# Where the first spectral fold stands at the seam of two MLP groups

## The chip, the cores and the metric

The kernel runs on one core of one Trainium2 chip. The metric is the device time of one execution in microseconds (us). TensorE does the matmuls, VectorE and ScalarE the element-wise work and all reads of PSUM, GpSimd element-wise work on SBUF, and SyncE issues the DMAs. Each engine works through its own instructions in the order in which they stand in the program. In the profile the engines are PE (with PEld for its weight loads), DVE, ACT, POOL and SP.

## The reference

```python
x = A_x                                    # 1 x 2048 x 448, float32
xn = layernorm(x)
# spectral branch (GFNet): 2-D real FFT, a complex weight, and back
y  = irfft2(rfft2(xn, axes=(-2, -1)) * (A_w_r + 1j * A_w_i), s=(2048, 448), axes=(-2, -1))
# S2-MLP branch
h  = gelu(layernorm(xn) @ w1)              # 448 -> 448
hs = shift(h, +1, -1, +2, -2 on the four channel quarters) @ w2
x1 = xn + hs
h2 = gelu(layernorm(x1) @ w3) @ w4         # 448 -> 1792 -> 448
out = x + y + (x1 + h2)
```

## The kernel before

All matmuls are done in float16 with each operand split into a high half and a low half, three products per matmul of the reference: high by high, high by low, low by high. So every operand is made by two instructions, a ScalarE copy that rounds to the high half, and a VectorE subtraction that leaves the low half. The 2048 tokens are 16 blocks of 128, block b holding the tokens with number b modulo 16, and they are called `xb(b)`.

The program runs in this order. First come the LayerNorm, `w1`, the shift and `w2`, block by block. `ln2` is the second LayerNorm: for a set of up to four blocks it takes statistics, subtracts the mean, scales to a high half (L481, ScalarE) and a low half (L482 and L484, VectorE: two column ranges) in the tile `y`, and transposes each block into `x2all` by a DMA (L486). The last call of it covers blocks 12 to 15.

Then the second MLP. It is cut into units (G, fp): G counts the eight pairs of blocks, fp the seven groups of 256 hidden channels. A unit has a front (`front`): 22 matmuls (L381) of 256 columns into one PSUM bank `pw`, then a gelu in place (L698, ScalarE), the high half `hf` (L700, ScalarE) and the low half (L701, VectorE). And it has a back (`back`): 12 matmuls (L720) of 448 columns into the two `acc` banks, of which 4 use only the high half of `hf` as weights first and the other 8 are placed where the low half is there too. After the seventh back of a G, VectorE adds `acc` to `xb` (L726). Units are queued as filler: `mlp` issues the front of a unit some units ahead of its back (`AH = 2` here), so TensorE always has a front to do while an `hf` is being made. `mlp([0])` forms the first group of units, (0,0) to (0,6); `mlp([1, 2])` the second, (1,0) to (2,6). The fronts use four PSUM banks in turn (tags `mm` and `tr`).

Beside the second group stands the first stage of the spectral branch. It works on eight pairs of blocks b0 = 0, 2, ... 14. `do_fold(b0)` loads the pair again from HBM into `xf` (L509; three buffers), normalizes it (L513, two ScalarE activations), copies one wrap-around column (L514), and lets GpSimd form sums and differences of the row with its mirror image (L519 and L520 into the shared row buffer `xr`, L522 twice into `f`). `step1_in` makes the halves `xh` of each block (L529 ScalarE, L530 VectorE; four buffers). `step1` is the first Fourier product of each block: 12 matmuls of 128 columns (L539) into a bank `ps` (tag `sp`, two buffers), evacuated by L543 (ScalarE) and L544 (VectorE) into `y1`. After all eight pairs the spectral middle (`chunk_a` to `chunk_c`) follows beside the units of G = 2 to 5, then the way back beside the last ones.

A scheduler that models the engines writes out the order of each engine from priorities. The second MLP's matmuls have the lowest priority, the evacuations of `front` the highest. On top of this the program pins instructions with `behind(key)`: what is issued inside may stand on its engine only after the named instruction. Two tables place the folds:

```python
with behind("f", *FOLD[b0 // 2]):      # do_fold: L513, L514 after hf of that unit
    ...
with behind("m", *PACE[b // 2]):       # step1 of both blocks after the back of that unit
    step1(b)
    step1(b + 1)
```

`("f", G, fp)` names L700 and L701 of a unit, `("m", G, fp)` the last matmul of its back. Other uses of the pins at the seam: `unscale` (L491 loads, L492) is pinned behind units of the second group by `EARLY`.

Of the kernel before, what the change touches and what calls it, by code (L numbers as in the profile page):

```python
# [29 lines left out]
VPRE = 2.0 ** -3  # L30
EPS = 1e-5
AH = 2
PACE = [(0, 6), (1, 1), (1, 2), (1, 4), (1, 5), (2, 0), (2, 1), (2, 3)]
FOLD = [(0, 5), (1, 0), (1, 1), (1, 3), (1, 4), (1, 6), (2, 0), (2, 2)]
PIN = [("a3",), ("a3",), ("a3",), ("a3",)]
WMAX = [(1, 4), (1, 5), (1, 6), (2, 0), (2, 1), (2, 2), (2, 3), (2, 4)]
HS = 3
# [82 lines left out]
def body(tc, nc, x, wf, w1, w2, w3, w4, c_g, c_n, c_small, out):  # L120
# [234 lines left out]
    @contextlib.contextmanager  # L355
    def behind(*key):
        key = key if len(key) > 1 else key[0]
        with contextlib.ExitStack() as st:
            for i in after[key]:
                st.enter_context(tc.issue_after(i))  # L360
            yield
# [145 lines left out]
    def do_fold(b0):  # L507
        X = pfd.tile([128, 2, D + 1], F32, tag="xf", bufs=3, name=f"xf{b0}")
        after["X", b0] = (SY.dma_start(X[:, :, 0:D], xv[:, b0:b0 + 2]).ins,)  # L509
        with behind("f", *FOLD[b0 // 2]):  # L510
            for i in range(2):
# [14 lines left out]
    def step1_in(b):  # L526
        f = folds.pop(b)
        t = xh_buf[b % 4]
        i = A.activation(out=t[:, 0:452], in_=f, func=AF.Copy)  # L529
        j = V.tensor_tensor(out=t[:, 452:904], in0=f, in1=t[:, 0:452], op=ALU.subtract)  # L530
        after["x", b] = i.ins, j.ins

    def step1(b):
        t = xh_buf[b % 4]
        pm = bank("sp", f"ps1_{b}")
        for q in range(4):
            for n, (xi, ri) in enumerate(PASS):
                o = xi * 452 + 113 * q
                T.matmul(pm[:, 128 * q:128 * q + 128], t[:, o:o + 128], cR[ri][:, 128 * (q % 2):128 * (q % 2) + 128],  # L539
                         start=n == 0, stop=n == 2)  # L540
        src = pm.rearrange("p (q h k) -> p q h k", h=2, k=4)
        y = [Ya[:, p, :, :, :, b, :].rearrange("p q c h k -> p (q c) h k") for p in range(2)]
        A.activation(out=y[0], in_=src, func=AF.Copy)  # L543
        V.tensor_tensor(out=y[1], in0=src, in1=y[0], op=ALU.subtract)  # L544
# [370 lines left out]
    for b in range(0, NB, 2):  # L915
        do_fold(b)
        step1_in(b)
        step1_in(b + 1)
        with behind("m", *PACE[b // 2]):
            step1(b)  # L920
# [61 lines left out]
```

## Time and profile before

| | |
|---|---|
| median of three runs | 416.20 us (416.14 to 416.21) |
| profiled execution | 416.43 us |
| its span | 414.6 us |
| mean granted TensorE clock | 0.999 of full speed |
| instructions | 8472 |
| matmuls | 3313 |
| bytes read from and written to HBM | 35.52 MB, 3.67 MB |

All times in the trace are counted from the start of the span of the profiled execution; 1.8 us of its time lie outside the span. A row of a timeline gives the start, the length from the first start to the last end, engine, line and operation, what is written from what, the shapes and the number of instructions merged in the row, and in brackets the idle time of the engine before it with what ended it. A row of groups gives the number of instructions, busy time, mean duration in ns, and idle time before them. A row of windows gives for each stretch its length and the busy time and count of PE, PEld, DVE, ACT and POOL, then the clock, the DMA share and the GB/s. A matmul's printed duration overlaps the next one's, so the cost of one is read from starts.

### The profile page before, as it was taken

The page shows a single profiled execution, that of the slowest core. Times are in us where ns is not written, and L with a number is a line of the kernel's source. Part 1 is how long each engine was busy: PE and PEld are TensorE (multiplying, and loading weights), DVE is VectorE, ACT ScalarE, POOL GpSimd, SP SyncE. Part 2 cuts the span into 40 slices and gives each one's busy share as a digit, 9 for nine tenths or more (in the row PEclk, how much of TensorE's full clock was granted, in tenths as well). Part 3 has the DMA queues.
Part 4 walks back from the last instruction along what each step waited for, and adds up shares of the span by engine and source line. Part 5 has one row for each costly group of instructions (what it writes and reads, how often), then busy time and mean ns, then how long its engine had stood idle before and what let it go on. Part 6 is the DMA issues. An engine that isn't in the chain of part 4 may idle for free.

```text
span 414.6 us, 8472 instructions
## 1 busy us (share of the span) xinstructions
PE 407.9 (98%) x3313; PEld 290.4 (70%) x3313; DVE 294.3 (71%) x613; ACT 246.1 (59%) x428; POOL 97.2 (23%) x172
## 2 busy tenths in 40 slices
PE   8999999999989999999999999999999999999996
PEld 3655555765658777776888887877777766777885
DVE  4888899798866879854799888857999934112122
ACT  4698879973758876643689888854344533222321
POOL 3876710102245947400021122110000000000000
PEclk9999999999999999999999999999999999999999
DMA  8959879914867557315256655500111011001001
GB/s 275 350 189 177 159 148 323 158 59 90 186 166 206 153 183 221 90 47 141 70 149 163 168 144 141 127 27 2 69 46 66 2 47 44 2 0 46 2 0 46
DMA packets 54536, 48.53 MB, mean 117 GB/s; under 512 B 37536, under 2 KB 48864, under 8 KB 54496
## 3 DMA queue, kind: packets, MB, share of 16 engines
q1 hardware_dynamic: 54496, 47.99, 43.6%
q8 instruction: 26, 0.43, 0.4%
q14 instruction: 14, 0.11, 0.1%
HBM read 35.52 MB, written 3.67 MB: 95 GB/s over the span
## 4 chain that ended last, share of the span: by engine, by line
PE 68%; DVE 12%; ACT 7%; issue 4%; DMA 4%; POOL 2%; SPq 1%; DVEq 0%; POOLq 0%; ACTq 0%
PE pw L381 26%; PE acc L720 25%; PE pw L410 4%; PE ps L539 3%; PE pe L663 2%; PE wps L749 2%; PE py L684 2%; ACT te L619 2%; DVE xt L452 2%; DMA x2mem<-y 2%; DMA x2mem<-w 1%; PE pu L642 1%; PE pp L597 1%; DVE y L484 1%; PE px L614 1%
## 5 line engine op out<-in xcount | busy, mean ns | idle before, releaser
L381 PE MATMUL pw<-x2mem,w3p 128*128 128x256 f16 x1232 | 151.7, 273 | 0.0
L720 PE MATMUL acc<-w4p,hf 128*128 128x448 f16 (+1 forms) x714 | 139.7, 341 | 1.4 <-DVE hf L701 1.4
L381 PEld LDWEIGHTS <-w3p 128*128 128x128 f16 x1232 | 119.0, 98 | 22.4
L720 PEld LDWEIGHTS <-hf 128*128 128x128 f16 x714 | 69.2, 98 | 49.9 <-DVE hf L701 1.8
L701 DVE SCALAR_TENSOR_TENSOR hf<-pw,h,hf 128x512 f16<-128x512 f32 x56 | 41.8, 747 | 64.1 <-ACT hf L700 63.7
L698 ACT ACTIVATE pw<-pw,pe 128x512 f32<-128x512 f32 x56 | 36.7, 656 | 76.8 <-PE pw L381 76.6
L450 PE MATMUL pw<-w2p,h 112*128 112x448 f16 x192 | 39.9, 352 | 0.7 <-DMA h<-hs 0.7
L700 ACT ACTIVATE hf<-pw,h 128x512 f16<-128x512 f32 x56 | 38.3, 687 | 1.5
L410 PE MATMUL pw<-w1p,xT 128*128 128x448 f16 x176 | 35.4, 352 | 0.0
L623 POOL TENSOR_TENSOR z<-te 128x450 f32<-128x450 f32 x16 | 15.7, 982 | 69.5 <-DVE te L621 69.5
L450 PEld LDWEIGHTS <-h 112*128 112x128 f16 x192 | 18.6, 98 | 17.2 <-DMA h<-hs 1.0
L410 PEld LDWEIGHTS <-xT 128*128 128x128 f16 x176 | 16.9, 98 | 16.4 <-DVE xT L375 0.8
L604 ACT ACTIVATE pf<-pp 64x450 f16<-64x450 f32 x32 | 17.4, 543 | 12.6 <-DVE pf L605 8.3
L605 DVE TENSOR_TENSOR pf<-pp,pf 64x450 f16<-64x450 f32 x32 | 19.9, 622 | 4.3 <-ACT pf L604 3.9
L522 POOL TENSOR_TENSOR f<-xr 128x452 f32<-128x452 f32 x16 | 18.4, 1173 | 0.6
L619 ACT ACTIVATE te<-px 64x450 f32<-64x450 f32 x32 | 17.3, 540 | 1.1 <-PE px L614 0.6
L726 DVE SCALAR_TENSOR_TENSOR xt<-acc,p,xt 128x448 f32<-128x448 f32 (+1 forms) x17 | 10.9, 651 | 8.6 <-PE acc L720 8.3
L530 DVE TENSOR_TENSOR xh<-f,xh 128x452 f16<-128x452 f32 x16 | 12.6, 828 | 5.5 <-ACT xh L529 5.5
L519 POOL TENSOR_TENSOR xr<-xf 128x452 f32<-128x452 f32 x8 | 9.9, 1236 | 26.0 <-issue 20.2
L529 ACT ACTIVATE xh<-f 128x452 f16<-128x452 f32 x16 | 8.4, 571 | 10.3 <-POOL f L522 10.2
L684 PE MATMUL py<-vh,csm 128*128 128x448 f16 x48 | 14.0, 352 | 0.0
L663 PE MATMUL pe<-csm,U 113*128 113x113 f16 (+1 forms) x192 | 13.7, 213 | 0.0
(164 smaller groups left out, 572.5 us busy)
## 6 DMA issues: line engine op xcount, KB each, us to landing
wc<-wf SPq DMA_DIRECT2D x32, 225.0 KB, 3.7
wl<-wf SPq DMA_DIRECT2D x8, 450.0 KB, 4.0
xt<-x SPq DMA_DIRECT2D x8, 448.0 KB, 9.0
xf<-x SPq DMA_DIRECT2D x8, 448.0 KB, 3.9
loads<-x SPq DMA_DIRECT2D x7, 448.0 KB, 3.7
out<-xt SPq DMA_DIRECT2D x13, 224.0 KB, 1.9
w3raw<-w SPq DMA_DIRECT2D x3, 896.0 KB, 13.7
gn<-c_g SPq DMA_DIRECT2D x16, 128.0 KB, 3.1
```

What stands on the lines that cost most here:

```text
L381: T.matmul(ps_out, wp[:, wi + t, cols], xT[:, xi + t, tok], start=t == 0 and wi + xi == 0, stop=t == 3 and wi == 4)
L410: T.matmul(pm[:, :D], xTs[g][:, xi + t, 128 * i:128 * i + 128], w1p[:, wi + t], start=t == 0 and p == 0, stop=t == 3 and p == 2)
L450: T.matmul(pm[:, :D], hT[g][:112, 4 * hi + k, o:o + 128], w2p[:, wi, k], start=n == 0, stop=n == 11)
L522: P.tensor_tensor(out=f[:, :, k:k + 2].rearrange("p b s d -> p s b d"), in0=u[:, :, 0], in1=u[:, :, 1], op=op)
L605: V.tensor_tensor(out=lo, in0=src, in1=hi, op=ALU.subtract)
L619: A.activation(out=e[64 * h:64 * h + 64], in_=px_[64 - 64 * h:128 - 64 * h, :2 * DF], func=AF.Copy)
L663: T.matmul(pe[:, 113 * q:113 * q + 113], U[b // 8 * 8][ui][:kd, q, b % 8, :], cI[ii][:kd, 113 * q:113 * q + 113], start=n == 0, stop=n == 2)
L684: T.matmul(py[:, :D], cV[ri], vh[:, vi], start=n == 0, stop=n == 2)
L698: A.activation(out=pm, in_=pm, func=AF.Gelu_apprx_tanh, scale=r3)
L700: i = A.activation(out=h[:, 0], in_=pm, func=AF.Copy, scale=h3)
L701: j = V.scalar_tensor_tensor(out=h[:, 1], in0=pm, scalar=h3, in1=h[:, 0], op0=ALU.mult, op1=ALU.subtract)
L720: m = T.matmul(to, h[:, hi, o:o + 128], w4p[0][:, wi, f, r], start=f == 0 and n == 0, stop=f == 13 and n == 2)
```

## The change

The first entries of both tables are moved: the fold of blocks 0 and 1 is pinned behind `hf` of unit (0,6), the last unit of the first group, where it was pinned behind that of unit (0,5). The products of these two blocks are pinned behind the back of unit (1,0), the first of the second group, where they were pinned behind the back of (0,6). All the other entries stay.

```diff
-PACE = [(0, 6), (1, 1), (1, 2), (1, 4), (1, 5), (2, 0), (2, 1), (2, 3)]
-FOLD = [(0, 5), (1, 0), (1, 1), (1, 3), (1, 4), (1, 6), (2, 0), (2, 2)]
+PACE = [(1, 0), (1, 1), (1, 2), (1, 4), (1, 5), (2, 0), (2, 1), (2, 3)]
+FOLD = [(0, 6), (1, 0), (1, 1), (1, 3), (1, 4), (1, 6), (2, 0), (2, 2)]
```

## The prediction

> **What bounds the kernel now.** I read the page's busy line and groups first, then the windows, then TensorE's own timeline around the change, then the three engines that feed it there.
>
> ```profile
> PE 407.9 (98%) x3313; PEld 290.4 (70%) x3313; DVE 294.3 (71%) x613; ACT 246.1 (59%) x428; POOL 97.2 (23%) x172
> ```
>
> ```profile
> L381 PE MATMUL pw<-x2mem,w3p 128*128 128x256 f16 x1232 | 151.7, 273 | 0.0
> L720 PE MATMUL acc<-w4p,hf 128*128 128x448 f16 (+1 forms) x714 | 139.7, 341 | 1.4 <-DVE hf L701 1.4
> L381 PEld LDWEIGHTS <-w3p 128*128 128x128 f16 x1232 | 119.0, 98 | 22.4
> ```
>
> TensorE is busy for 98% of the span. The page warns that matmul ends are modelled, so I don't take that share alone as proof; the last column matters more. Of the two largest groups, L381 never finds TensorE idle, and L720 does for 1.4 us in all, waiting for the second half of `hf` (VectorE, L701). The windows say where that is:
>
> ```profile
> 117.96:130.39 12.43, 11.07 (x103) 8.81 (x102) 8.94 (x12) 7.38 (x14) 5.01 (x6) 1.00 0.75 185
> 130.39:215.00 84.61, 84.61 (x783) 64.56 (x781) 64.27 (x94) 54.11 (x96) 35.22 (x32) 1.00 0.48 140
> 215.00:255.00 40.00, 39.83 (x430) 32.87 (x428) 34.65 (x57) 32.96 (x60) 8.84 (x9) 1.00 0.58 148
> ```
>
> The first window holds PE for 11.07 of 12.43 us: the whole 1.4 us lies there, at the seam between the first MLP group and the second, which is where the change works. The 84.6 us behind it are full. In the spectral stretch from 215 to 255, where VectorE and ScalarE are also close to full, TensorE is idle for only 0.17 us. So TensorE sets the time from the seam on, and time won at the seam is carried to the end unless a new wait takes it.
>
> ```profile
> 113.42 4.70 PE L720 MATMUL acc<-w4p,hf 128*128 128x448 f16 x24
> 117.96 0.71 PE L381 MATMUL pw<-x2mem,w3p 128*128 128x256 f16 x5
> 118.58 0.93 PE L720 MATMUL acc<-w4p,hf 128*128 128x448 f16 x4
> 120.87 1.69 PE L720 MATMUL acc<-w4p,hf 128*128 128x448 f16 x8 [1.35 <-DVE hf L701]
> 122.39 1.25 PE L381 MATMUL pw<-x2mem,w3p 128*128 128x256 f16 x10
> 123.70 1.39 PE L539 MATMUL ps<-csm,xh 128*128 128x128 f16 x22
> 124.93 5.62 PE L381 MATMUL pw<-x2mem,w3p 128*128 128x256 f16 x50
> 130.39 2.43 PE L720 MATMUL acc<-w4p,hf 128*128 128x448 f16 x12
> ```
>
> From starts to starts, a front matmul (L381) costs (130.39 - 124.93)/50 = 0.109 us, a back matmul (L720) (117.96 - 113.42)/24 = 0.189, a fold product (L539) (124.93 - 123.70)/22 = 0.056. The back of the last unit, (0,6), starts its four first-half matmuls at 118.58 and its eight second-half ones at 120.87. Four cost 0.76, so 2.29 - 0.76 = **1.53 us** are lost. The five front matmuls ahead took 0.62 where five cost 0.55: another **0.07**, waiting for the first half. The stall is worth 1.60 us, 0.25 more than the printed 1.35, because the printed idle time begins at the modelled end.
>
> Why `hf` of (0,6) is late stands in ScalarE's, VectorE's and GpSimd's rows:
>
> ```profile
> 112.26 0.69 ACT L700 ACTIVATE hf<-pw,h 128x512 f16<-128x512 f32 x1
> 113.52 1.41 ACT L513 ACTIVATE xf<-xf,nm,vw 128x448 f32<-128x448 f32 x2 [0.57 <-DMA xf<-x]
> 114.84 2.33 ACT L481 ACTIVATE y<-y,vs 128x448 f16<-128x448 f32 x4
> 117.08 0.19 ACT L514 ACTIVATE xf<-xf 128x2 f32<-128x2 f32 x1
> 117.17 0.63 ACT L698 ACTIVATE pw<-pw,pe 128x512 f32<-128x512 f32 x1
> 117.84 0.69 ACT L700 ACTIVATE hf<-pw,h 128x512 f16<-128x512 f32 x1
> 121.97 1.05 ACT L529 ACTIVATE xh<-f 128x452 f16<-128x452 f32 x2 [3.44 <-POOL f L522]
> 126.48 0.69 ACT L700 ACTIVATE hf<-pw,h 128x512 f16<-128x512 f32 x1
> 127.07 1.41 ACT L513 ACTIVATE xf<-xf,nm,vw 128x448 f32<-128x448 f32 x2
> ```
>
> ```profile
> 112.98 0.75 DVE L701 SCALAR_TENSOR_TENSOR hf<-pw,h,hf 128x512 f16<-128x512 f32 x1 [0.65 <-ACT hf L700]
> 115.53 0.28 DVE L482 SCALAR_TENSOR_TENSOR y<-y,vs 128x64 f16<-128x64 f32 x1 [1.79 <-ACT y L481]
> 115.73 0.61 DVE L484 SCALAR_TENSOR_TENSOR y<-y,vs 128x384 f16<-128x384 f32 x1
> 116.26 0.28 DVE L482 SCALAR_TENSOR_TENSOR y<-y,vs 128x64 f16<-128x64 f32 x1
> ...
> 117.71 1.08 DVE L482 SCALAR_TENSOR_TENSOR y<-y,vs 128x64 f16<-128x64 f32 x1
> 118.72 1.43 DVE L484 SCALAR_TENSOR_TENSOR y<-y,vs 128x384 f16<-128x384 f32 x1
> 120.07 0.74 DVE L701 SCALAR_TENSOR_TENSOR hf<-pw,h,hf 128x512 f16<-128x512 f32 x1
> ...
> 134.73 2.40 DVE L530 TENSOR_TENSOR xh<-f,xh 128x452 f16<-128x452 f32 x2 [1.64 <-ACT xh L529]
> ```
>
> ```profile
> 117.35 1.36 POOL L519 TENSOR_TENSOR xr<-xf 128x452 f32<-128x452 f32 x1 [5.62 <-ACT xf L514]
> ...
> 119.81 2.12 POOL L522 TENSOR_TENSOR f<-xr 128x452 f32<-128x452 f32 x2
> 129.27 1.06 POOL L519 TENSOR_TENSOR xr<-xf 128x452 f32<-128x452 f32 x1 [7.33 <-issue]
> ...
> 131.43 2.65 POOL L522 TENSOR_TENSOR f<-xr 128x452 f32<-128x452 f32 x2
> ```
>
> The first fold delays (0,6) twice. On ScalarE, L513 waits for its DMA and then runs, so the four `y` casts (L481) of the last LayerNorm start at 114.84 instead of right behind L700. And GpSimd's fold starts while VectorE still has the fourth `y` pair: that pair takes 120.07 - 117.71 = 2.36 us, the first took 116.26 - 115.53 = 0.73.
>
> **The change, step by step.** The built order shows no instruction added or removed, and the queues of GpSimd and SyncE stay as they are. On ScalarE, fold 0's L513 and L514 move behind L700 of (0,6). On TensorE the 24 products of pair 0 move from the middle of unit (1,0)'s front to behind the back of (1,0). Their evacuations move along: L543 and L544, formerly ahead of (1,0)'s gelu, come after (1,2)'s `hf`, L543 split around two L529 and L544 around the L530 pair of fold 2.
>
> *Unit (0,6).* L481 can follow L700 at 112.26 + 0.59 (the spacing 126.48 to 127.07) = 112.85; four take 117.08 - 114.84 = 2.24, to 115.1. L698 starts there, L700 0.67 later (117.17 to 117.84) at 115.8, done at 116.5. VectorE is in L701 until 113.7, then four pairs of 0.73, to 116.6, then L701: the second half at 117.4. TensorE wants the halves at 118.3 and 119.2 (three front matmuls of (1,0) come first, and a fourth between; 117.96 + 0.33; + 0.76 + 0.11). Both are there with 1.8 us to spare, so the 1.60 us vanish. If the fourth pair still cost 2.36, the second half would come at 119.0, still in time.
>
> [...]
>
> *Fold 0.* L513 starts at 115.8 + 0.6 = 116.4, L514 1.4 later, GpSimd at 118.1 instead of 117.35. It took 119.81 + 2.12 - 117.35 = 4.58, so `f` is there at 122.7. Behind L529 on ScalarE now stands unit (1,0)'s gelu: this is the added wait. TensorE ends that front at 119.2 + 1.51 (eight back matmuls) + 18 x 0.109 = 122.6; two L529 hold the gelu until 123.7, about 1 us late. Then L700 at 124.4, L701 at 125.1, second half at 125.8. TensorE wants them at 122.6 + 44 x 0.109 = 127.4 and 128.2. Cover 2.4 us: free.
>
> *The products.* TensorE reaches pair 0's products at 127.4 + 12 x 0.189 = 129.7, long after L530. End of the moved block: 129.7 + 24 x 0.056 = 131.0. In the profile of before the same instructions end at 130.39 + 2.27 = 132.7. The difference is 1.6, as the stall says.
>
> *Fold 2, the thinnest place.* ScalarE reaches its L513 at 125.0 instead of 127.07, 2.1 earlier, so all of fold 2 comes 2.1 earlier: `f` at 131.43 + 2.65 - 2.1 = 132.0, the L530 pair from 132.6 to 135.0, and L544 of `ps1_1`, now behind that pair and taken like L701 at 0.74 (both pass 512 columns), ends at 135.7. TensorE comes to pair 2's products at 131.0 + 22 x 0.109 + 2.27 = 135.7; the second tile, which needs the bank that L544 empties, starts 0.67 later, at 136.4. Slack about 0.7 us. Free, but not by much.
>
> Sum: -1.53 - 0.07 = **-1.60 us**. The profiled execution took 416.43 us with a span of 414.6; its own time becomes 414.83. The median of the three runs is 0.23 below the profiled execution, so the forecast is 416.2 - 1.6 = **414.6 us**.
>
> **The rivals.**
> *Part of it goes into fold 2's slack.* If GpSimd holds each L530 of that pair for a whole L522 of 1.33 us (half of 2.65), and each then runs 0.7 (an estimate from L484's 0.61 for 384 columns, at 452), the pair takes 4.1 instead of 2.40 and ends at 136.7, L544 at 137.4, and TensorE waits 1.0 us: **415.6**. Against it: 2.40 was measured in just this overlap with the next fold. Chance 0.08.
>
> *No change: TensorE isn't what sets the time.* [...] The trace speaks against it: in a run of 22 front and 12 back matmuls without any wait, 34 loads of 0.098 us lie in 22 x 0.109 + 12 x 0.189 = 4.67 us, 71%: that is the share when TensorE issues without pause. What could absorb the win is the spectral stretch, if VectorE's chain there bound; its 0.17 us of idle TensorE says it doesn't. Price: the whole 1.6, **416.2**. Chance 0.06.
>
> *Slower: the gelu of (1,0) stuck behind L529.* ScalarE serves in order, so if GpSimd's fold came late, the hold would reach TensorE as a stall at the back of (1,0), and then all later folds slip. It decides once the fold is over 2.4 us later than worked out, and makes the kernel slower once it is over 4.0 late; by 5.0 the time is **417.2**. For it: ScalarE already waited 3.44 us there. [...] Chance 0.05.
>
> **How the numbers follow.** Forecast 0.81, the rivals 0.08, 0.06 and 0.05. The forecast's own spread is about 0.4 us: rounding of starts, and the small idle times later that any shift reshuffles. The range takes this below (414.2) and reaches through the first rival above (415.6). A measurement of this kernel can tell about 0.2%, 0.83 us: faster means under 415.37. That takes in the forecast and half of the first rival (its hold may be less than a whole L522), 0.85; the other half and the second rival lie within 0.2%, 0.10; slower 0.05.
>
> **What would show it.** In the changed profile: no idle time before L720 at the seam; L701 of (0,6) from about 116.7 instead of 120.07; the fourth `y` pair at about 0.7 us; GpSimd's fold 0 from about 118; the twelve matmuls of (1,0)'s back from 127.4; pair 2's products unpaused. I am wrong if TensorE shows a wait of over 0.8 us anywhere from 118 to 145, or if the seam is gained and TensorE idles later by as much.

## Result, and the profile after

The changed kernel takes 414.76 us (median of 11 runs, 414.70 to 415.19) against 415.96 us before (11 runs, 415.26 to 416.21). The ratio is 0.9974, with a 95% interval of 0.9964 to 0.9983: about 1.1 us less (415.96 x 0.0026; 0.7 to 1.5), and the medians are 1.2 us apart. The profiled execution took 414.82 us with a span of 413.0, 1.6 less than the span of the profile before.

The group of the back matmuls and the same windows as before (per row: length; busy and count of PE, PEld, DVE, ACT, POOL; clock; DMA share; GB/s):

```profile
L720 PE MATMUL acc<-w4p,hf 128*128 128x448 f16 (+1 forms) x714 | 139.6, 341 | 0.0
```

```profile
117.96:130.39 12.43, 12.43 (x103) 9.46 (x102) 7.63 (x9) 7.46 (x14) 7.77 (x8) 1.00 0.78 196
130.39:215.00 84.61, 84.61 (x798) 65.28 (x796) 61.24 (x95) 53.97 (x96) 31.56 (x31) 1.00 0.45 134
215.00:255.00 40.00, 39.83 (x423) 32.53 (x421) 34.60 (x56) 33.43 (x62) 7.99 (x9) 1.00 0.64 158
```

The 1.4 us of idle time before L720 have become 0.0, the seam's window is full, and nothing has opened behind it: the spectral stretch keeps its 0.17 us. TensorE's timeline of the changed kernel at the seam:

```profile
117.98 0.49 PE L381 MATMUL pw<-x2mem,w3p 128*128 128x256 f16 x3
118.31 0.92 PE L720 MATMUL acc<-w4p,hf 128*128 128x448 f16 x4
119.06 0.27 PE L381 MATMUL pw<-x2mem,w3p 128*128 128x256 f16 x1
119.17 1.68 PE L720 MATMUL acc<-w4p,hf 128*128 128x448 f16 x8
120.68 6.93 PE L381 MATMUL pw<-x2mem,w3p 128*128 128x256 f16 x62
127.45 2.43 PE L720 MATMUL acc<-w4p,hf 128*128 128x448 f16 x12
129.72 1.50 PE L539 MATMUL ps<-csm,xh 128*128 128x128 f16 x24
131.06 2.56 PE L381 MATMUL pw<-x2mem,w3p 128*128 128x256 f16 x22
...
135.73 1.50 PE L539 MATMUL ps<-csm,xh 128*128 128x128 f16 x24
```

The seam begins where it did before (117.98 against 117.96), the second-half matmuls follow the fourth front matmul without a pause, and the moved block ends at 131.06 where the same work ended at 132.66 (130.39 + 2.27) before: 1.60 us. ScalarE, VectorE and GpSimd of the changed kernel:

```profile
112.53 2.33 ACT L481 ACTIVATE y<-y,vs 128x448 f16<-128x448 f32 x4
...
121.87 1.05 ACT L529 ACTIVATE xh<-f 128x452 f16<-128x452 f32 x2 [4.21 <-POOL f L522]
122.85 0.66 ACT L698 ACTIVATE pw<-pw,pe 128x512 f32<-128x512 f32 x1
```

```profile
115.50 0.28 DVE L482 SCALAR_TENSOR_TENSOR y<-y,vs 128x64 f16<-128x64 f32 x1
115.70 0.61 DVE L484 SCALAR_TENSOR_TENSOR y<-y,vs 128x384 f16<-128x384 f32 x1
116.23 0.75 DVE L701 SCALAR_TENSOR_TENSOR hf<-pw,h,hf 128x512 f16<-128x512 f32 x1
...
134.12 0.68 DVE L544 TENSOR_TENSOR y<-ps,y 128x512 f16<-128x512 f32 x1
```

```profile
117.74 1.06 POOL L519 TENSOR_TENSOR xr<-xf 128x452 f32<-128x452 f32 x1 [6.31 <-ACT xf L514]
...
119.91 1.93 POOL L522 TENSOR_TENSOR f<-xr 128x452 f32<-128x452 f32 x2
```

The casts start 2.3 us earlier, the fourth `y` pair takes 116.23 - 115.50 = 0.73 us instead of 2.36, and `hf` is complete at 116.98 instead of 120.81. GpSimd starts its fold only 0.4 us later than before, but by then the pairs are over.

### The profile page after: what moved, and what is told of

It is laid out like the page before. It is cut to its first block, busy times and chain, and to the rows that moved or that the text cites. A ratio compares the mean times of both kernels' runs of the same rounds, so it can differ in the third digit from the quotient of the medians.

```text
span 413.0 us, 8472 instructions
## 1 busy us (share of the span) xinstructions
PE 406.8 (98%) x3313; PEld 290.2 (70%) x3313; DVE 289.5 (70%) x613; ACT 245.4 (59%) x428; POOL 95.2 (23%) x172
## 4 chain that ended last, share of the span: by engine, by line
PE 85%; DVE 5%; ACT 5%; DMA 2%; issue 2%; POOL 1%; SPq 0%; POOLq 0%; DVEq 0%
PE pw L381 30%; PE acc L720 28%; PE pw L450 9%; PE pw L410 6%; PE ps L539 3%; PE pe L663 2%; PE py L684 2%; ACT te L619 2%; PE pu L642 1%; PE pp L597 1%; PE px L614 1%; DVE te L621 1%; DMA xt<-x 1%; DVE sta L289 1%; ACT zb L630 1%
## 5 line engine op out<-in xcount | busy, mean ns | idle before, releaser
L381 PE MATMUL pw<-x2mem,w3p 128*128 128x256 f16 x1232 | 151.1, 273 | 0.0
L720 PE MATMUL acc<-w4p,hf 128*128 128x448 f16 (+1 forms) x714 | 139.6, 341 | 0.0
L381 PEld LDWEIGHTS <-w3p 128*128 128x128 f16 x1232 | 119.1, 98 | 22.1
L720 PEld LDWEIGHTS <-hf 128*128 128x128 f16 x714 | 69.3, 98 | 48.1
L701 DVE SCALAR_TENSOR_TENSOR hf<-pw,h,hf 128x512 f16<-128x512 f32 x56 | 41.8, 748 | 66.8 <-ACT hf L700 66.4
L700 ACT ACTIVATE hf<-pw,h 128x512 f16<-128x512 f32 x56 | 38.3, 686 | 1.5
L522 POOL TENSOR_TENSOR f<-xr 128x452 f32<-128x452 f32 x16 | 16.4, 1046 | 0.6
L519 POOL TENSOR_TENSOR xr<-xf 128x452 f32<-128x452 f32 x8 | 9.7, 1218 | 26.6 <-issue 20.3
L663 PEld LDWEIGHTS <-U 113*128 113x128 f16 (+1 forms) x192 | 11.9, 97 | 2.4
L620 DVE SCALAR_TENSOR_TENSOR te<-px,sc,wc 128x450 f32<-128x450 f32 x16 | 11.0, 684 | 3.7 <-ACT te L619 3.6
```

Of the source, the lines that this page charges most:

```text
L381: T.matmul(ps_out, wp[:, wi + t, cols], xT[:, xi + t, tok], start=t == 0 and wi + xi == 0, stop=t == 3 and wi == 4)
L663: T.matmul(pe[:, 113 * q:113 * q + 113], U[b // 8 * 8][ui][:kd, q, b % 8, :], cI[ii][:kd, 113 * q:113 * q + 113], start=n == 0, stop=n == 2)
L700: i = A.activation(out=h[:, 0], in_=pm, func=AF.Copy, scale=h3)
L701: j = V.scalar_tensor_tensor(out=h[:, 1], in0=pm, scalar=h3, in1=h[:, 0], op0=ALU.mult, op1=ALU.subtract)
L720: m = T.matmul(to, h[:, hi, o:o + 128], w4p[0][:, wi, f, r], start=f == 0 and n == 0, stop=f == 13 and n == 2)
```

## Experiments

Open were: which half of the change matters; whether ScalarE's delay of the casts or the overlap of the fold with the fourth pair was dear; why the timed gain is 1.1 us when the two spans differ by 1.6; and what the overlap of GpSimd and VectorE costs by itself. Where an edit moves lines, line numbers of rows differ by a few from the kernel's: L380 below is the kernel's L381, and L475 is an added line.

**The fold alone (e1_fold_only).**

```diff
-FOLD = [(0, 5), (1, 0), ...
+FOLD = [(0, 6), (1, 0), ...
```

> Only the fold is moved behind (0,6); pair 0's products stay pinned behind the back of (0,6), and the scheduler now puts them into the front of (1,1). Theory (the win is the seam stall, caused by the fold's place; where the products stand is free): seam stall gone, the products come at about 123.8 us when the first block's halves are there, no new idle TensorE time; time as the changed kernel, 1.1 to 1.6 us under before. Rival (the products' new place is what helps): no change against before, 416.0.

Measured: 414.96 us, 0.9975 of before (0.9965 to 0.9985). TensorE's timeline:

```profile
120.83 3.33 PE L381 MATMUL pw<-x2mem,w3p 128*128 128x256 f16 x29
124.00 0.28 PE L539 MATMUL ps<-csm,xh 128*128 128x128 f16 x2
```

The scheduler puts the products after 29 fronts, where they wait for nothing (120.83 + 29 x 0.109 = 123.99). The fold alone brings the whole gain, and the products' new pin adds nothing that can be measured.

**The products alone (e2_products_only).**

```diff
-PACE = [(0, 6), (1, 1), ...
+PACE = [(1, 0), (1, 1), ...
```

> Only the products are moved behind the back of (1,0); the fold stays behind (0,5). Theory: the stall before the second-half matmuls of (0,6) stays at 1.4 to 1.5 us printed or as large as before has it in this run; time as before, within 0.3 us. Rival (the products' place): about 1.1 us faster.

Measured: 415.88 us, 0.9999 of before (0.9990 to 1.0008): the time is as expected. The stall is there, but its printed size is 0.97 us where 1.4 to 1.5 was expected:

```profile
118.52 0.92 PE L720 MATMUL acc<-w4p,hf 128*128 128x448 f16 x4
120.41 1.69 PE L720 MATMUL acc<-w4p,hf 128*128 128x448 f16 x8 [0.97 <-DVE hf L701]
```

By starts, 120.41 - 118.52 - 0.76 = 1.13 us are lost. The rival, that the products' place is what helps, falls.

**ScalarE's delay kept, the overlap taken away (e3b_wrap_late).** The products are moved as in the run above, and of the fold only the small copy that GpSimd waits for:

```diff
             for i in range(2):
                 ...
-            A.activation(out=X[:, :, D:D + 1], in_=X[:, :, 0:1], func=AF.Copy)
+        with behind("f", *(FOLD[b0 // 2] if b0 else (0, 6))):
+            A.activation(out=X[:, :, D:D + 1], in_=X[:, :, 0:1], func=AF.Copy)
```

> As the run with the products moved alone, but the one small ScalarE copy that GpSimd's fold waits for (the wrap-around column) is pinned behind hf of (0,6); the two normalizations stay ahead of the y casts and keep their wait for the DMA. So ScalarE's delay of the casts stays and the overlap of GpSimd's fold with the fourth y pair goes. Theory (the overlap is the price): first half of hf at 118.5, four y pairs of 0.73 us each, second half at 119.2, TensorE short by 0.1 us at most; time within 0.2 us of the changed kernel. Rival (ScalarE's delay is the price): the stall stays above 1 us, time as before.

Measured: 414.89 us, 0.9973 of before (0.9963 to 0.9983). Rows of ScalarE, VectorE and TensorE:

```profile
114.93 2.33 ACT L481 ACTIVATE y<-y,vs 128x448 f16<-128x448 f32 x4
```

```profile
117.80 0.28 DVE L482 SCALAR_TENSOR_TENSOR y<-y,vs 128x64 f16<-128x64 f32 x1
118.00 0.61 DVE L484 SCALAR_TENSOR_TENSOR y<-y,vs 128x384 f16<-128x384 f32 x1
118.55 0.75 DVE L701 SCALAR_TENSOR_TENSOR hf<-pw,h,hf 128x512 f16<-128x512 f32 x1
```

```profile
118.36 0.60 PE L381 MATMUL pw<-x2mem,w3p 128*128 128x256 f16 x4
118.80 2.43 PE L720 MATMUL acc<-w4p,hf 128*128 128x448 f16 x12
```

The casts start as late as in the first profile by the time of the trace (114.93 against 114.84). TensorE comes 0.4 us later to the seam here (118.36 against 117.96), so the casts lie 3.43 us ahead of it, where they lie 3.12 ahead in the first profile and 3.58 ahead (114.39 and 117.97) in the run with the products alone, which stalls. The fourth pair takes 0.75 us, and TensorE runs through all twelve back matmuls. So without the overlap there is no stall: ScalarE's delay costs nothing by itself, or at most the 0.07 us that the first half of `hf` was late in the first profile. What the delay did was to use up the slack that would have hidden the overlap.

**The kernel before once more (e4_before_again).**

> The kernel before, unchanged, for a second profile: the first profile has a stall of 1.60 us at the seam, the timed runs differ by 1.1 to 1.2. Theory (the stall's size differs from execution to execution, since the fold's start hangs on the landing of its DMA and so does the overlap): this profile shows a stall of another size, between 0.7 and 1.6 us, and its span differs from the changed kernel's by about that. Rival (something else than the stall gives back 0.4 us later): stall 1.60 again, while the times are 1.1 apart.

Measured: 415.68 us (12 runs, 414.92 to 416.32), 0.9994 of before (0.9985 to 1.0003), span 413.9. Its seam:

```profile
112.74 1.42 ACT L513 ACTIVATE xf<-xf,nm,vw 128x448 f32<-128x448 f32 x2 [0.24 <-DMA xf<-x]
```

```profile
118.40 0.92 PE L720 MATMUL acc<-w4p,hf 128*128 128x448 f16 x4
120.09 1.69 PE L720 MATMUL acc<-w4p,hf 128*128 128x448 f16 x8 [0.77 <-DVE hf L701]
```

The stall is 120.09 - 118.40 - 0.76 = 0.93 us by starts. The same instructions in the same order lose 1.53, 1.13 (in the run with the products alone, whose seam is the same) and 0.93 us in three profiled executions. The fold's L513 starts 1.26, 1.23 and 0.92 us behind L700's start there, and waits 0.57, 0.54 and 0.24 us for its DMA. In the first two that start hardly differs, and the rest came with ScalarE being 0.4 us earlier as a whole (L513 at 113.07 in the run with the products alone against 113.52). The overlap itself doesn't vary, though the expectation says so: the fourth pair takes 2.36 us in all three (117.71 to 120.07, 117.25 to 119.61, 116.93 to 119.29). What varies is when it comes. So the stall's size is a property of the execution, and the 1.1 us of the timed runs agree with it. The three spans agree too: 414.6, 414.2 and 413.9 lie 1.6, 1.2 and 0.9 us over the 413.0 of the changed kernel. Three profiles show this; they don't give its distribution, and why ScalarE is earlier as a whole in two of them stays open.

**Four more GpSimd additions beside the pairs (d4_pool_busy).** From here on the edit is made to the changed kernel:

```diff
+        for _ in range(4 if b0 == 12 else 0):
+            P.tensor_tensor(out=xr[:, 0:D], in0=o[1][:, 0], in1=o[1][:, 0], op=ALU.add)
         V.tensor_scalar(out=a, in0=mv[:, :n, 1], scalar1=eps12, ...
```

> The changed kernel with four more GpSimd additions of 448 columns (their result is used by nobody) behind the mean subtractions of the last LayerNorm, so that GpSimd reads SBUF from about 111.4 to 115.5 us beside the first y pairs; the other engines' orders stay. Theory (a GpSimd addition and a VectorE y pair exclude each other): a pair beside GpSimd takes about 2.1 us instead of 0.73, so the four pairs end about 1.4 us later than in the changed kernel, and the second half of hf of (0,6) is there at 118.3, before TensorE wants it at 119.2. No stall, time as the changed kernel. Rival (the fourth pair was slow for another reason): pairs of 0.73, time as the changed kernel.

Measured: 414.82 us, 0.9972 of before (0.9961 to 0.9982): no stall, as expected. Rows of ScalarE and VectorE:

```profile
113.63 2.34 ACT L481 ACTIVATE y<-y,vs 128x448 f16<-128x448 f32 x4 [1.13 <-DVE vs L282]
```

```profile
117.92 0.74 DVE L701 SCALAR_TENSOR_TENSOR hf<-pw,h,hf 128x512 f16<-128x512 f32 x1
```

Only the first pair met the additions and took 1.42 us (114.33 to 115.75), not 2.1. The casts came 1.1 us late instead, because the small VectorE operations that make their scale were held too: two of them took 0.80 and 0.79 us beside the additions, where they take 0.16 alone. By time this run can't tell the theories apart, but a pair of 1.42 us beside GpSimd already speaks against the rival's 0.73. It shows one thing more: `hf` is complete at 117.92 + 0.74 = 118.66, 1.7 us later than in the changed kernel, and TensorE doesn't wait. The overlap of the kernel before adds 2.36 - 0.73 = 1.63 us to the pair, so by this sum it would have been hidden without ScalarE's delay (116.98 + 1.63 = 118.61, against 119.17 when TensorE wants it): neither of the two makes the stall alone.

**Eight additions (d8_pool_busy).** `range(8 ...)` in the same place.

> The same with eight additions, to about 119.7 us, and the fold right behind them. Theory (exclusion): all four pairs beside GpSimd at about 2.1 us each, from 113.3 to 121.6, second half of hf at 122.4, a stall of 2.8 to 3.5 us before the second-half matmuls of (0,6) where TensorE wants it at 119.2; time about 3.1 us over the changed kernel, 417.9. Rival (another reason): pairs of 0.73, no stall, and the fold's two us of lateness hidden: time as the changed kernel.

Measured: 416.44 us, 1.6 over the run with four on the same chip, and 1.0013 of before (1.0004 to 1.0021). The expectation missed by half: the pairs beside GpSimd took 1.40 us, not 2.1.

```profile
116.28 0.95 DVE L482 SCALAR_TENSOR_TENSOR y<-y,vs 128x64 f16<-128x64 f32 x1
117.16 0.61 DVE L484 SCALAR_TENSOR_TENSOR y<-y,vs 128x384 f16<-128x384 f32 x1
117.68 0.95 DVE L482 SCALAR_TENSOR_TENSOR y<-y,vs 128x64 f16<-128x64 f32 x1
```

```profile
119.15 0.27 PE L380 MATMUL pw<-x2mem,w3p 128*128 128x256 f16 x1
119.88 1.69 PE L720 MATMUL acc<-w4p,hf 128*128 128x448 f16 x8 [0.46 <-DVE hf L701]
...
136.46 0.83 PE L539 MATMUL ps<-csm,xh 128*128 128x128 f16 x12
137.98 0.22 PE L539 MATMUL ps<-csm,xh 128*128 128x128 f16 x1 [0.69 <-DVE y L544]
```

One of the two instructions of a pair is held, not both: here L482 takes 0.95 us where it took 0.28 in the changed kernel, and L484 keeps its 0.61. TensorE loses 119.88 - 119.15 - 0.11 = 0.62 us at the seam. And because the fold came 3 us late, the second tile of pair 2's products waited for L544, 137.98 - 136.46 - 12 x 0.056 = 0.85 us. This is the prediction's thinnest place, but not its first rival: the L530 pair of fold 2 takes 2.39 us, no longer than before, and starts late (134.93 against 131.83) because the late first fold held ScalarE and with it the later folds, which is the chain of the slow rival. A third wait for L544 follows at 160.41, behind 12 back matmuls from 157.74: 160.41 - 157.74 - 12 x 0.189 = 0.40 us. The three make 1.87 us, and the span is 1.9 longer than with four additions (415.0 against 413.1).

**Eight additions without a gap (d8_no_gap).** Each addition above writes the same range and waits for the one ahead. Now they write two ranges in turn:

```diff
-            P.tensor_tensor(out=xr[:, 0:D], ...
+            P.tensor_tensor(out=xr[:, 452 * (j % 2):452 * (j % 2) + D], ...
```

> As the run with eight additions, but they write the two halves of the row buffer in turn, so that none waits for the one just before it, as the fold's own two additions L519 and L520 do. In the run before, where each waited for its predecessor, a y pair cost 1.40 us, in the first profile beside the fold 2.36. Theory (VectorE gets in only at a gap between two GpSimd instructions; without a gap L482 and L484 of a pair each wait out one): pairs of 2.0 to 2.4 us, second half of hf of (0,6) at about 122, a stall of 2.5 to 3.2 us there and, with the fold about 2 us late, little more behind; time 417.4 to 418.4. Rival (the pair beside the fold was dear for another reason than a missing gap): pairs of 1.40 and a time of 416.4 as in the run before.

Measured: 421.38 us, 1.0140 of before (1.0121 to 1.0159): over the expected range. VectorE, GpSimd, TensorE, and windows from the seam on:

```profile
114.25 1.05 DVE L482 SCALAR_TENSOR_TENSOR y<-y,vs 128x64 f16<-128x64 f32 x1
115.22 1.30 DVE L484 SCALAR_TENSOR_TENSOR y<-y,vs 128x384 f16<-128x384 f32 x1
116.44 0.95 DVE L482 SCALAR_TENSOR_TENSOR y<-y,vs 128x64 f16<-128x64 f32 x1
```

```profile
111.61 7.79 POOL L475 TENSOR_TENSOR xr<-y 128x448 f32<-128x448 f32 x8
```

```profile
119.16 0.27 PE L380 MATMUL pw<-x2mem,w3p 128*128 128x256 f16 x1
123.09 3.17 PE L720 MATMUL acc<-w4p,hf 128*128 128x448 f16 x8 [3.65 <-DVE hf L701]
126.05 8.18 PE L380 MATMUL pw<-x2mem,w3p 128*128 128x256 f16 x62
134.06 2.43 PE L720 MATMUL acc<-w4p,hf 128*128 128x448 f16 x12
```

```profile
119.40:123.00 3.60, 0.04 (x1) 0.00 (x0) 3.60 (x5) 0.00 (x0) 3.52 (x4) 0.83 0.60 116
123.00:126.00 3.00, 2.91 (x8) 1.20 (x9) 0.72 (x2) 1.05 (x2) 1.16 (x2) 0.50 0.88 230
126.00:128.50 2.50, 2.50 (x13) 1.77 (x12) 1.76 (x3) 0.00 (x0) 0.00 (x0) 0.50 1.11 303
128.50:131.00 2.50, 2.50 (x24) 2.21 (x23) 0.12 (x1) 1.50 (x3) 0.00 (x0) 0.98 0.26 87
```

The eight additions now take 7.79 us instead of 9.44, and a pair takes 116.44 - 114.25 = 2.19: both its instructions are held (1.05 us instead of 0.28, 1.30 instead of 0.61). The next two take 2.10 and 2.23. So the pairs are as the theory of the gap has them. The rows of GpSimd in the run before and in the first profile show the gap and its absence:

```profile
115.83 1.32 POOL L475 TENSOR_TENSOR xr<-y 128x448 f32<-128x448 f32 x1
117.23 2.72 POOL L475 TENSOR_TENSOR xr<-y 128x448 f32<-128x448 f32 x2
```

```profile
118.67 1.06 POOL L520 TENSOR_TENSOR xr<-xf 128x452 f32<-128x452 f32 x1
```

In the run before, an addition ends at 117.15 and the next starts at 117.23; L484 starts in between, at 117.16, and is not held (0.61 us). In the first profile L520 starts at 118.67, ahead of the end of L519 at 118.71, and L484, which starts at 118.72, is held (1.43 us). So the 2.36 us of the first profile fit the price of a fold whose L519 and L520 follow each other without a gap.

The stall is 123.09 - 119.16 - 0.11 = 3.82 us, 0.6 over the expectation; the casts' scale was held as well (L281 took 0.80 us and L282 0.85, each 0.16 in the changed kernel), and the casts start 0.8 us later than in the run before (113.55 against 112.77). The span is 419.6 us, 6.6 longer than the changed kernel's, and the rest of that was not expected at all: the granted clock is halved, 0.50 in the windows from 123.00 to 128.50. The first window's mean of 0.83, taken as 1.00 first and 0.50 then, puts (1 - 0.83) x 2 x 3.60 = 1.2 us of it at half clock, so the clock fell at about 121.8, when TensorE had been idle for about 2.3 us (its last matmul ends at 119.16 + 0.27 = 119.43). By the 0.98 of the last window it came back at about 128.6. The 8 back matmuls take 126.05 - 123.09 = 2.96 us instead of 1.51, and the 62 front ones 134.06 - 126.05 = 8.01 instead of 6.77. That is 2.7 us, and with the stall 6.5.

## Why the prediction was right

*What bounds the kernel.* Right. The span fell by what the seam lost, 1.60 us, and the added waits of the last runs reached the end of the kernel as well (1.87 of 1.9 us with eight additions, 6.5 of 6.6 without a gap).

*Unit (0,6).* Right step by step: L701 at 116.23 (116.7 was worked out), the fourth pair at 0.73, no pause. The prediction says that the first fold delays (0,6) twice, and the runs show how the two go together: it takes both to make the stall. With the delay kept and the overlap gone there is none (e3b_wrap_late), and the four additions show 1.7 us of lateness hidden when the delay by L513 is gone, which agrees with the prediction's 119.0 for a fourth pair that still costs 2.36. The kernel before with its overlap and without the delay was not run.

*Fold 0.* The place is right, the size was too dark. Without the overlap GpSimd needs 119.91 + 1.93 - 117.74 = 4.10 us, not 4.58, so L529 follows at 121.87 and the gelu of (1,0) starts 0.2 us late (122.85, its front ending at 120.68 + 18 x 0.109 = 122.64), not 1 us. The cover of 2.4 us was 127.45 - 124.23 = 3.2 (L700 of (1,0) ends at 123.54 + 0.69). The slow rival was 0.8 us further off.

*The products and fold 2.* The block ended at 131.06 (131.0) and pair 2's products came at 135.73 (135.7). L544 of the thin place ended at 134.80, so its slack was 1.6 us instead of 0.7; that the place is real shows in the run with eight additions. The first rival's longer hold didn't come: the L530 pair took 2.36 us, where fold 0's, with no GpSimd work beside it, took 1.17 (from 122.48). That GpSimd holds each L530 for a whole L522 was the author's estimate, and no run shows it.

*The sum.* The step that was mis-sized is the term -1.60 us. It was read from one execution and taken for all; the timed runs give about -1.1, and the three seams give 1.53, 1.13 and 0.93 us at the second half. The first profile was among the slower executions, 416.43 against a median of 415.96 over the 11 runs. Within its own execution the sum is right: 416.43 - 1.60 = 414.83, and the profiled execution of the changed kernel took 414.82. Taking the 1.60 off the median of three other executions was the weak step. That 414.6 lies within 0.2 us of 414.76 all the same is partly luck: the base of 416.20 was 0.24 above the median of the 11 runs, the gain 0.40 above the 1.20 between the medians, and the two errors offset in part. That the stall varies and then goes away shows in the spread as well: the changed kernel's runs spread over 0.5 us, those of the kernel before over 1.0.

*The second rival.* It didn't come: the time fell. The share of weight loads is 70% in both profiles, while TensorE's idle time at the seam went from 1.4 us to none. As a measure of what was left to win here the share says nothing; the last column of the groups did.

## What to carry to other kernels

In a stretch that TensorE fills, look for the one idle entry before a matmul group, and walk back from it until you find not only who was late but what made the late instruction long. Here a VectorE pair was three times as long because GpSimd ran beside it (2.36 us; 0.73 in the changed kernel, where it didn't), and it was enough to let GpSimd start once the pairs were over. Size such a stall from several executions, not from one.

## What was not expected of the hardware

In these runs, what a `y` pair loses beside GpSimd hangs on gaps in GpSimd's own stream: a pair of 0.73 us alone takes 1.40 beside additions that each wait for the one ahead, and 2.19 beside additions that don't. In the run with the gaps the held L482 at 116.28 ends at 117.23, just behind the addition that ends at 117.15, and the L484 behind it takes its 0.61 us. Without a gap VectorE loses again at the next instruction: L484 takes 1.30. L701, which reads one operand from PSUM, keeps 0.74 to 0.75 us in the same stretches (0.75 at 112.69 and 0.74 at 119.09 with eight additions, 0.74 at 113.38 without a gap). Why the `y` instructions are held and L701 isn't, no run shows.

A long pause of TensorE had a second price. Stalls of 0.6 to 1.5 us left the granted clock at 1.00 (1.53 us before, in the window 117.96:130.39; 0.93 in e4_before_again, 117.85:129.61; 0.62 and 0.85 with eight additions, 117:130 and 130:145). In the one of 3.65 us it fell about 2.3 us into the pause, and the half clock, 0.50 in two windows, lasted from about 121.8 to about 128.6, 5.5 us beyond the restart at 123.09, and cost another 2.7 us. One run shows this; how short a pause can be and still halve the clock, and what sets the 2.3 and the 6.8 us, it doesn't show.
